# Two-layer memory attention with SwiGLU: attention matmuls issued in pairs on the two 64-row halves of the tensor array

## The chip, the cores and the metric

The kernel runs on one core of one Trainium2 chip. The metric is the device time of one execution in microseconds; the table below gives the runs of the kernel before. TensorE (PE) does the matmuls and writes into PSUM, which has eight banks of 128 partitions by 512 float32 columns. VectorE (DVE) and ScalarE (ACT) read PSUM, GpSimd (POOL) works on SBUF only, and SyncE (SP) issues nearly all DMAs. Every engine runs its own instructions in the order in which they were written; semaphores tie the engines together.

## The reference, cut to what matters

Two layers, each an attention block with a compressive memory and then a SwiGLU block, both with a layer norm before and the residual added after. S = 2048 rows, D = 512, H = 32 heads of 16, N = 4 segments of L = 512 rows, F = 1792.

```python
for s in range(N):
    qs, ks, vs = q[:, :, s], k[:, :, s], v[:, :, s]
    logits = jnp.einsum("bhqd,bhkd->bhqk", qs, ks) * scale + mask
    p = _softmax(logits, axis=-1)
    a_dot = jnp.einsum("bhqk,bhkd->bhqd", p, vs)
    pq = phi(qs)
    num = jnp.einsum("bhld,bhde->bhle", pq, M)
    den = jnp.einsum("bhld,bhd->bhl", pq, z)[..., None] + 1e-6
    o = g * (num / den) + (1.0 - g) * a_dot
    pk = phi(ks)
    M = M + jnp.einsum("bhld,bhle->bhde", pk, vs)
    z = z + jnp.einsum("bhld->bhd", pk)
```

## The kernel before, in words

**Precision.** Each float32 operand is split into a high part and a remainder, both held as fp32r. A product is the sum of three: high by high, high by remainder, remainder by high.

**Units.** An attention layer has 32 units: 4 segments, 4 groups of 8 heads, and the even or the odd four heads of the group. A unit does the following.

- `load3` (L513) brings q and k of the unit from DRAM scratch. Four heads lie as two pairs: index `j` picks partitions 0 to 47 or 64 to 111, index `p` a slot in the free dimension. The 48 partitions are the three terms of the split, 16 dimensions each. `cq` has four slots `2*j+p` in which the other half's partitions stay zero; `ck` has two.
- `mx_units` (L545) computes logits with queries on the partitions, to get the row maxima. Per head it fills three banks: 256+256 columns for query tiles 0 and 1, 384 for tile 2, 512 for tile 3. All 127 partitions take part, and since `cq` is zero in the other half, one matmul gives one head. DVE reduces each block with the causal mask (L564) into `mx`. `fin` transposes `mx` on PE (L573), ACT negates it into `nm` (L575), and a DMA on ACT's queue writes it to partition 127 of `cq`, against a partition of ones in `ck`.
- `at_units` (L585): `lt` computes the transposed logits (keys on the partitions) for 10 blocks of key tile by query tile, two matmuls of 256 columns each (L609). ACT takes the exponential (L615), POOL masks the four diagonal blocks (L619). `pv` multiplies by v on four 32-column quarters of the array, one per head (L636). `post` transposes and normalises on DVE.

**The other attention work on PE.** `mm3` (L298) issues the 12 matmuls of 128x512 of one tile (L295); it serves `qk_proj` (L481), `v_proj` (L465) and `wo_proj` (L732). `ln_transpose` (L384) transposes a normalised row tile in four matmuls (L387). `mem_read` (L682), `mem_update` (L702) and the end of `post` have memory products and transposes of their own (L690, L706, L667).

**SwiGLU.** `ffn` (L847) does the first block of weight columns directly (`up`, L1007; for row blocks 0 and 1 already during the attention), and the others by a Strassen scheme: `strassen` (L1029, matmuls at L1047) and `down` (L1084, matmuls at L1091).

**What sets the order.** Nothing is issued when it is described. Each call records an operation with its engine, a cost, what it reads and writes, and a priority. `issue` (L151) then replays them: the engine that can start earliest by the recorded costs takes its ready operation with the lowest priority number. Priorities come from tables of offsets (`OFF`, `PRE`, `EP`) and step constants. `bank` takes one of the eight PSUM banks when an operation first needs it; `CAP` limits how many banks each class of user may hold. `DRAIN` is what the replay adds where PE changes between full-array and quarter operations.

## Time and profile before

| | us |
|---|---|
| median of 3 runs | 1878.33 |
| lowest and highest run | 1873.25, 1881.59 |
| the profiled execution, its own time | 1878.99 |
| span of the profiled execution (first to last instruction) | 1877.2 |
| PE busy in the span | 1825.3 |
| DVE busy | 1407.5 |
| ACT busy | 873.1 |
| POOL busy | 918.9 |

Busy time is the time in which at least one instruction of the engine was under way. Matmuls overlap in the pipeline, so the length of one matmul (some 400 ns for 512 columns) is not its cost; the distance from one start to the next is. In the profile's views PE is the matmul, PEld the weight load, x is a count, and an arrow names what ended an idle time.

### The profile page before, as it was taken

The numbers are of one execution on the slowest core, as the hardware profiler recorded it, in microseconds if no ns is written. First come the engines' busy times: TensorE is split into PE (matmuls) and PEld (weight loads), VectorE is DVE, ScalarE is ACT, GpSimd is POOL, SyncE is SP. The second block draws the span as 40 slices with busy tenths as digits, with TensorE's granted clock in tenths as the row PEclk, the third lists the DMA queues.
The fourth block names the chain that finished last, engine by engine and source line by source line (L and its number), as shares of the span: only waits on it lengthen the run. The fifth ranks groups of instructions, "written<-read, shape, count | busy, mean of one in ns | idle before, by whom it ended". The sixth has DMA issues, their size and how long they took to land.

```text
span 1877.2 us, 33021 instructions
## 1 busy us (share of the span) xinstructions
PE 1825.3 (97%) x11360; PEld 1450.6 (77%) x11360; DVE 1407.5 (75%) x3834; ACT 873.1 (47%) x1629; POOL 918.9 (49%) x1186
## 2 busy tenths in 40 slices
PE   7999999999999999999989999999999999999999
PEld 5787787877778887788867877778777788878887
DVE  6878788778876678766776777787898766796656
ACT  4565564555533432433345655556454433333432
POOL 6344444444655654647533444444446647445551
PEclk9999999999999999999999999999999999999999
DMA  7535444464232132111373353455642311312121
GB/s 236 148 102 147 135 133 144 144 214 119 74 119 61 46 91 89 52 50 57 114 217 101 106 163 115 130 167 140 188 124 74 123 51 56 94 64 57 44 58 45
DMA packets 126967, 206.14 MB, mean 110 GB/s; under 512 B 14160, under 2 KB 52048, under 8 KB 126800
## 3 DMA queue, kind: packets, MB, share of 16 engines
q1 hardware_dynamic: 124752, 203.49, 36.7%
q8 instruction: 91, 1.49, 0.3%
q10 hardware_dynamic: 2048, 0.53, 0.1%
q14 instruction: 76, 0.62, 0.1%
HBM read 136.34 MB, written 67.11 MB: 108 GB/s over the span
## 4 chain that ended last, share of the span: by engine, by line
PE 48%; DVE 7%; issue 2%; DMA 2%; POOL 1%; ACT 1%; SPq 0%; DVEq 0%; POOLq 0%; ACTq 0%
PE ps L1047 18%; PE ps L1091 10%; PE ps L295 7%; PE ps L636 3%; PE ps L558 3%; PE ps L609 3%; DVE junk L564 2%; DMA s<-nm 1%; PE ps L1017 1%; DVE tt L961 1%; DVE s L983 1%; DVE s L1096 1%; PE ps L387 1%; DVE mx L564 0%; DVE of L961 0%
## 5 line engine op out<-in xcount | busy, mean ns | idle before, releaser
L1047 PE MATMUL ps<-s,s 128*128 128x512 f32 x2016 | 547.3, 396 | 9.5 <-ACT s L982 4.6
L295 PE MATMUL ps<-s,s 128*128 128x512 f32 x1536 | 526.2, 407 | 2.7 <-ACT s L451 1.2
L564 DVE CUSTOM_DVE_ANT_0 junk<-ps,amask 128x128 bf16<-128x128 f32 (+3 forms) x1024 | 433.5, 484 | 46.5 <-PE ps L558 45.1
L1047 PEld LDWEIGHTS ps<-s,s 128*128 128x128 f32 x2016 | 376.7, 188 | 106.0 <-ACT s L982 6.7
L1091 PE MATMUL ps<-s,vt 128*128 128x512 f32 x1296 | 378.0, 397 | 2.2 <-ACT vt L1003 2.2
L295 PEld LDWEIGHTS ps<-s,s 128*128 128x128 f32 x1536 | 287.2, 191 | 51.6 <-issue 6.1
L615 ACT ACTIVATE s<-ps 128x512 f32<-128x512 f32 x448 | 253.9, 609 | 108.5 <-PE ps L609 97.2
L1091 PEld LDWEIGHTS ps<-s,vt 128*128 128x128 f32 x1296 | 245.2, 189 | 58.6 <-ACT vt L1003 2.6
L558 PE MATMUL ps<-ck,s 127*128 127x256 f32 (+2 forms) x1024 | 276.6, 334 | 5.7 <-DMA ck<-scrk 4.9
L609 PE MATMUL ps<-s,ck 128*128 128x256 f32 x1280 | 250.6, 287 | 6.4 <-DMA s<-nm 4.5
L609 PEld LDWEIGHTS ps<-s,ck 128*128 128x128 f32 x1280 | 221.3, 189 | 38.3 <-issue 4.9
L1096 DVE TENSOR_TENSOR s<-s,ps 128x512 f32<-128x512 f32 x224 | 150.1, 683 | 92.0 <-PE ps L1091 91.7
L619 POOL TENSOR_SCALAR_AFFINE_SELECT s<-s 128x512 f32<-128x512 f32 x192 | 126.8, 663 | 171.9 <-ACT s L615 166.6
L558 PEld LDWEIGHTS ps<-ck,s 127*128 127x128 f32 x1024 | 177.6, 189 | 28.8 <-issue 6.4
L914 POOL TENSOR_TENSOR s<-mem,s 128x512 fp32r<-128x512 f32 x96 | 130.7, 1362 | 0.0
L492 POOL TENSOR_SCALAR s<-raw 128x512 fp32r<-128x512 f32 x64 | 45.4, 709 | 173.9 <-ACT raw L491 163.6
L1017 PE MATMUL ps<-s,s 128*128 128x512 f32 x384 | 123.9, 400 | 0.9 <-ACT s L391 0.9
L921 POOL COPY turn<-vt 128x1 f32<-128x1 f32 x20 | 3.7, 186 | 235.6 <-DVE vt L1004 235.6
L636 PE MATMUL ps<-s,vt 128*32 128x384 f32 (+3 forms) x1536 | 115.7, 419 | 0.1
L636 PEld LDWEIGHTS ps<-s,vt 128*32 128x32 f32 x1536 | 43.3, 109 | 64.1 <-issue 46.2
L615 ACT ACTIVATE pc<-ps 128x512 f32<-128x512 f32 x128 | 78.7, 615 | 19.9 <-PE ps L609 19.3
L494 POOL TENSOR_TENSOR s<-raw,s 128x512 fp32r<-128x512 f32 x64 | 84.3, 1317 | 4.3
(172 smaller groups left out, 2585.3 us busy)
## 6 DMA issues: line engine op xcount, KB each, us to landing
s<-scrq SPq DMA_DIRECT2D x128, 192.0 KB, 3.5
ck<-scrk SPq DMA_DIRECT2D x128, 192.0 KB, 4.5
scrq<-s SPq DMA_DIRECT2D x32, 512.0 KB, 3.6
scrk<-s SPq DMA_DIRECT2D x32, 512.0 KB, 3.3
scrq<-s SPq DMA_DIRECT2D x32, 256.0 KB, 3.2
scrk<-s SPq DMA_DIRECT2D x32, 256.0 KB, 2.5
s<-xmid SPq DMA_DIRECT2D x32, 256.0 KB, 5.2
xin<-xmid SPq DMA_DIRECT2D x32, 256.0 KB, 2.7
```

What stands on the lines that cost most here:

```text
L295: pe(n, passes, lambda: nc.tensor.matmul(view(ps.ap), lhsT=av(a.ap), rhs=bv(b.ap), start=start, stop=stop), [(a, rk[0]), (b, rk[1])], [ps])
L558: nc.tensor.matmul(ps.ap[:, a * 256:a * 256 + nk], lhsT=cq.ap[0:127, 2 * j + p, qt * 128:(qt + 1) * 128], rhs=ck.ap[0:127, p, 0:nk], start ...
L564: dve(w, lambda a=a, qt=qt, w=w, ps=ps, junk=junks[qt % 2]: nc.vector.tensor_tensor_reduce(out=junk.ap[:, :w], in0=ps.ap[:, a * 256:a * 25 ...
L609: nc.tensor.matmul(ps.ap[:, 256 * p:256 * p + 256], lhsT=ck.ap[:, p, kt * 128:kt * 128 + 128], rhs=cq.ap.rearrange("r (j p) c -> r p j c", ...
L615: act(512, lambda: nc.scalar.activation(view().rearrange("p x i c -> p (x i c)"), ps.ap, AF.Exp, scale=SCALE), [ps], [(Pb, key)], table="exp")
L619: gp(0.593, lambda: nc.gpsimd.affine_select(out=view()[:, 0], in_=view()[:, 0], pattern=[[0, 4], [1, 128]], compare_op=OP.is_ge, fill=0.0, ...
L636: nc.tensor.matmul(ps.ap[32 * i:32 * i + 32, qt * 128:(qt + k) * 128], lhsT=vt.ap[:, kt, VW * hd:VW * hd + 32], rhs=view(k=k)[:, :, idx], ...
L914: gp(n / 400, lambda hi=hi, lo=lo, src=src: nc.gpsimd.tensor_sub(lo(), src(), hi().bitcast(F32)), [read, (wt, (o0, 0))], [(wt, (o0, 1))])
L1017: pe(512, 1, lambda i=i, j=j, kc=kc, x=x, ps=ps, wt=wt: nc.tensor.matmul(ps.ap, lhsT=wt.ap[:, i, kc, cs], rhs=XT[b][j].ap[:, :, kc], start ...
L1047: pe(512, 1, lambda i=i, kc=kc, x=x, buf=buf, view=view: nc.tensor.matmul(ps.ap, lhsT=w.ap[:, o, i, kc], rhs=view(buf.ap, kc), start=(x == 0),
L1091: pe(512, 1, lambda i=i, j=j, fi=fi, x=x, ps=ps, wt=wt, cs=cs: nc.tensor.matmul(ps.ap, lhsT=ht.ap[:, 0:2048].rearrange("p (f a c) -> p f a ...
L1096: dve(512, lambda ps=ps, t=t: nc.vector.tensor_add(xb.ap[:, t, :], xb.ap[:, t, :], ps.ap), [ps, (xb, t)], [(xb, t)])
```

## The change

**Logits.** One tile per unit (`cqk`, `[128, 2, 2, 512]`) now holds q and k; the partitions 0 to 47 hold one head and 64 to 111 another, and nothing is zero-padded. Each matmul uses only 48 or 49 partitions of one half, and the matmuls come in pairs, the lower half for head `j=0` into one bank and the upper half for `j=1` into another. The rows of maxima go to partitions 48 and 112 of q, against -1 in k, so ACT copies `mx` without a sign. Transposed logits are cut by key tile, from the diagonal to column 512.

**Projections.** `mm_pair` takes two tiles at once (q and k of a group, or two row tiles of v or of the output). Twelve pair-steps use rows 0 to 63 for the first tile and 64 to 127 for the second; then the halves change places for twelve more. Between the two passes stands a hand-off: an ACT instruction that does nothing waits for the last matmul of the first pass, and the first matmul of the second pass waits for it. The same hand-off stands between the two transposes of `fin`. The first direct block of SwiGLU columns for row blocks 0 and 1 goes through `mm_pair` too.

**Transposes and the memory product** work on 64-row halves, two banks at once. `CAP`, the offsets, and the step constants are new, and `DRAIN` has entries for the halves ("lanes"); the replay's rule for banks counts several of one class in one operation.

```diff
-CAP = {'pj': 3, 'plt': 3, 'pmx': 3, 'ppv': 3, 'ff': 6, 'st': 6}
+CAP = {'pj': 4, 'plt': 4, 'pmx': 4, 'ppv': 2, 'ff': 6, 'st': 6}
...
-DRAIN = {("full", "cols"): 0.097, ("cols", "full"): 0.147}
+DRAIN = {("full", "cols"): 0.097, ("cols", "full"): 0.147, ("full", "lanes"): 0.2, ("lanes", "full"): 0.2,
+         ("lanes", "cols"): 0.096, ("cols", "lanes"): 0.22}
...
+    HALF = ((0, 64), (64, 128))
...
+    def mm_pair(ps, seqs):
+        got = {}
+        for ph in range(2):
+            n = len(seqs[0])
+            for x in range(n):
...
+                def go(x=x, ph=ph):
+                    for lane in range(2):
+                        q = lane ^ ph
+                        a, _, av, b, _, bv = seqs[q][x]
+                        r0, r1 = HALF[lane]
+                        o = nc.tensor.matmul(ps[q].ap, lhsT=av(a.ap)[r0:r1], rhs=bv(b.ap)[r0:r1],
+                                             start=(ph == 0 and x == 0), stop=(ph == 1 and x == n - 1))
+                        if ph == 1 and x == 0 and lane == 0:
+                            fence(o, got["turn"], "halves")
+                    got["last"] = o
+                pe(512, 1, go, rd, list(ps), mode="lanes", cost=0.229)
...
+                def bounce():
+                    got["turn"] = nc.scalar.nop()
+                    fence(got["turn"], got["last"], "halves")
+                turn = op("act", 0.06, bounce)
...
         def mx_units(u):
...
+            def part(cost, blocks):
+                ps = [bank("pmx"), bank("pmx")]
+                def fill():
+                    for p, qt, c0 in blocks:
+                        nk = 128 * (qt + 1)
+                        for j in range(2):
+                            nc.tensor.matmul(ps[j].ap[:, c0:c0 + nk],
+                                             lhsT=cqk.ap[64 * j:64 * j + 48, 0, p, qt * 128:(qt + 1) * 128],
+                                             rhs=cqk.ap[64 * j:64 * j + 48, 1, p, 0:nk], start=True, stop=True)
...
+            return [lambda p=p: part(0.232, ((p, 3, 0),)) for p in range(2)] + \
+                [lambda p=p: part(0.235, ((p, 2, 0), (p, 0, 384))) for p in range(2)] + \
+                [lambda: part(0.29, ((0, 1, 0), (1, 1, 256))), fin]
...
+            def part(b, cost, blocks, outs):
+                ps, Pb = [bank("plt"), bank("plt")], p_of(b)
+                def fill():
+                    for p, kt, c0 in blocks:
+                        nq = 512 - 128 * kt
+                        for j in range(2):
+                            nc.tensor.matmul(ps[j].ap[:, c0:c0 + nq],
+                                             lhsT=cqk.ap[64 * j:64 * j + 49, 1, p, kt * 128:(kt + 1) * 128],
+                                             rhs=cqk.ap[64 * j:64 * j + 49, 0, p, 128 * kt:512], start=True, stop=True)
```

**How the order moves.** The first place is PE in the middle of layer 0, where a unit's logits stand among projections. Before (L609 transposed logits, L558 logits for the maxima, L295 a projection; ps is a PSUM bank, s a large SBUF tile, ck the k tile):

```order
L609 MATMUL ps_4305<-s_211,ck_222 128x256 x2
L295 MATMUL ps_4266<-s_2665,s_120 128x512
L558 MATMUL ps_4312<-ck_90,s_67 128x256 x2
L558 MATMUL ps_4316<-ck_90,s_67 128x384
L558 MATMUL ps_4318<-ck_90,s_67 128x512
```

After (L615 logits for the maxima, L308 a projection, L632 the two transposes of `fin`):

```order
L308 MATMUL ps_4014<-s_230,s_3053 128x512
L615 MATMUL ps_4130<-s_238 128x384
L615 MATMUL ps_4131<-s_238 128x384
L615 MATMUL ps_4130<-s_238 128x128
L615 MATMUL ps_4131<-s_238 128x128
L632 MATMUL ps_4139<-ident,mx_578 16x64 x2
L308 MATMUL ps_4151<-s_3346,s_106 128x512
L308 MATMUL ps_4152<-s_3346,s_113 128x512
```

Five matmuls for one head's maxima and one block of another product have become pairs on two banks each; every projection step is two matmuls.

The second place is PE at a hand-off between the two passes of a projection (L308); the wait on ACT's sequencer is the hand-off, and L774 is the memory product:

```order
L308 MATMUL ps_2673<-s_1113,s_106 128x512
L308 MATMUL ps_2674<-s_1113,s_113 128x512
L615 MATMUL ps_2751<-s_67 128x256 [waits DMAHW7_49,DMAHW5_49,DVE_49]
L615 MATMUL ps_2752<-s_67 128x256 [waits DMAHW6_49,DMAHW1_49,DVE_49]
L308 MATMUL ps_2674<-s_1102,s_113 128x512 [waits Activation_sequencer_49]
L308 MATMUL ps_2673<-s_1102,s_106 128x512
L774 MATMUL ps_2763<-mb_265,phiq_2435 128x68 [waits Activation_49]
```

Four matmuls, two pair-steps, stand between the end of the first pass and the wait. Of the 72 paired projections 15 have nothing between, 8 up to one step, 25 about two steps, and the others three or more. Of the 64 in `fin`, 4 have nothing between, 4 one step, 13 two, the others more.

The third place is PE where layer 0's attention gives way to SwiGLU. Before (L295 the output projection, L1017 and L1047 SwiGLU):

```order
L295 MATMUL ps_6889<-s_238,s_5838 128x512
L1017 MATMUL ps_6896<-s_6483,s_4848 128x512
L295 MATMUL ps_6889<-s_224,s_5860 128x512
L1017 MATMUL ps_6929<-s_6480,s_5000 128x512
L1047 MATMUL ps_6886<-s_6766,s_6251 128x512
```

After (L308 pairs on halves, L1157 the Strassen products on the full array):

```order
L308 MATMUL ps_7703<-s_240,s_6664 128x512
L1157 MATMUL ps_7790<-s_7650,s_7027 128x512
L308 MATMUL ps_7702<-s_240,s_6664 128x512
L308 MATMUL ps_7703<-s_240,s_6664 128x512
L1157 MATMUL ps_7790<-s_7650,s_7027 128x512
L308 MATMUL ps_7702<-s_230,s_6679 128x512
```

The two kinds still alternate, but each alternation is now a change between halves and the full array. In the whole order PE changes from halves to the full array 55 times and back 55 times, and between halves and quarters 64 times each way; before, it changed between the full array and quarters 64 times each way. Inside SwiGLU the sequence of products is nearly the one before.

More of the change, by code (lines that the diff above doesn't have):

```diff
@@ L187, in issue @@
                             fr = sorted(free[tag])[:len(new)]
-                            if len(fr) < len(new) or not all(turn[b.cls] for b in new):
+                            many = [(c, [b.cls for b in new].count(c)) for c in {b.cls for b in new}]
+                            if len(fr) < len(new) or any(len(turn[c]) < k for c, k in many):
                                 heapq.heappop(n)
@@ L191, in issue @@
                                 continue
-                            when = max([fr[-1][0]] + [min(turn[b.cls]) for b in new])
+                            when = max([fr[-1][0]] + [sorted(turn[c])[k - 1] for c, k in many])
                             if when > t[e] + 1e-9:
@@ L316, in infini_swiglu @@
     bet = sb("bet", [128, NG, 2])
+    mxs = [sb(f"mx_{i}", [128, 16]) for i in range(2)]
     Mb = [sb(f"mb{n}", [128, 8, VW]) for n in range(NG)]
@@ L642, in pv @@
                 del MU[:]
-                pe(1280 + 100 * len(MU_), 4, go, [(vt, c) for c in range(8)] + reads + [e[1] for e in MU_],
-                   [ps] + [e[2] for e in MU_], mode="cols")
+                pe(1280 + 100 * len(MU_), 4, go, [(vt, c) for c in range(8)] + [f_[b] for b in range(3)] +
+                   [e[1] for e in MU_], [ps] + [e[2] for e in MU_], mode="cols")
                 for _, _, pm in MU_:
@@ L675, in post, with second, first, third @@
                        [of, (th, n)], [(tl, n)])
-            units = [lt(0, q) for q in range(4)] + [lt(1, q) for q in (1, 2, 3)]
-            units += [lt(2, 2), lt(3, 3), lt(2, 3), pv]
-            units.append(post)
-            return units
+            def second(p):
+                part(1, 0.235, ((p, 1, 0), (p, 3, 384)), (p,))
+                if p:
+                    tri(1, 0)
+                    tri(1, 384)
+            def first(p):
+                part(0, 0.232, ((p, 0, 0),), (p,))
+                if p:
+                    tri(0, 0)
+            def third():
+                part(2, 0.29, ((0, 2, 0), (1, 2, 256)), (0, 1))
+                tri(2, 0)
+            return [lambda p=p: first(p) for p in range(2)] + [lambda p=p: second(p) for p in range(2)] + \
+                [third, pv, post]
         def mem_read(s, n):
@@ L765, in attention @@
             at(-2.05)
-            for t in range(4):
-                ln_fin(0, t, "st")
+            for p in range(2):
+                ln_fin(0, p, "st")
         else:
```

463 lines of the change are left out of this document (251 added, 212 removed).

## The prediction

> **What bounds the kernel now.** I read the stretches of the span first, then the groups by line, then the timeline of one unit. The windows below are start, attention of layer 0, SwiGLU, attention of layer 1, SwiGLU; the columns are length, then busy time of PE, PEld, DVE, ACT and POOL.
>
> ```profile
> 0.00:52.00 52.00, 37.10 (x155) 29.12 (x155) 35.61 (x109) 22.68 (x39) 28.36 (x50) 0.97 0.78 232
> 52.00:456.00 404.00, 398.67 (x3344) 316.84 (x3345) 317.87 (x1231) 225.92 (x446) 173.32 (x262) 1.00 0.49 144
> 456.00:985.00 529.00, 513.19 (x2366) 409.22 (x2365) 390.96 (x717) 213.74 (x378) 295.59 (x335) 0.99 0.29 88
> 985.00:1425.00 440.00, 432.15 (x3586) 340.21 (x3584) 341.62 (x1295) 249.35 (x484) 192.73 (x297) 1.00 0.47 134
> 1425.00:1877.20 452.20, 444.15 (x1918) 355.24 (x1916) 321.45 (x488) 161.37 (x283) 228.86 (x245) 1.00 0.22 67
> 430.00:450.00 20.00, 19.10 (x143) 15.11 (x139) 18.79 (x85) 7.76 (x17) 4.37 (x6) 1.00 0.41 106
> ```
>
> In the two attention windows, 844 us together, PE is busy for 830.8 (98.4%) and DVE for 659.5 (78%). PE bounds them, and DVE is the next engine, with a fifth of slack. The last row is the one stretch I found where both are loaded: DVE 94%, PE 95.5%.
>
> ```profile
> L564 DVE CUSTOM_DVE_ANT_0 junk<-ps,amask 128x128 bf16<-128x128 f32 (+3 forms) x1024 | 433.5, 484 | 46.5 <-PE ps L558 45.1 <-issue 0.2
> L558 PE MATMUL ps<-ck,s 127*128 127x256 f32 (+2 forms) x1024 | 276.6, 334 | 5.7 <-DMA ck<-scrk 4.9 <-issue 0.2 <-ACT s L391 0.2
> L609 PE MATMUL ps<-s,ck 128*128 128x256 f32 x1280 | 250.6, 287 | 6.4 <-DMA s<-nm 4.5 <-DVE mx L564 0.6 <-ACT s L615 0.6
> ```
>
> The logits (L558, L609) are the work on PE that the change shrinks, and the idle time before them is 12 us in all: PE is not waiting for inputs there, it is computing. The maxima on DVE (L564), 433.5 us in the whole span, stay as they are.
>
> **Logits.** PE in the middle of a unit, start and length:
>
> ```profile
> 435.94 0.40 PE L558 MATMUL ps<-ck,s 127*128 127x256 f32 x2
> 436.18 0.40 PE L295 MATMUL ps<-s,s 128*128 128x512 f32 x1
> 436.41 0.34 PE L558 MATMUL ps<-ck,s 127*128 127x384 f32 x1
> 436.59 0.65 PE L609 MATMUL ps<-s,ck 128*128 128x256 f32 x4
> 437.07 0.40 PE L558 MATMUL ps<-ck,s 127*128 127x512 f32 x1
> 437.30 0.40 PE L609 MATMUL ps<-s,ck 128*128 128x256 f32 x2
> ```
>
> From start to start, two matmuls of 256 columns cost 0.24 us, 384 columns 0.18, 512 columns 0.23. The maxima of a head cost 0.24 + 0.18 + 0.23 = 0.65, of four heads 2.6; the ten transposed blocks cost 0.24 each, 2.4. That is 5.0 us for each of 64 units, 320 in all. After the change either product of a unit is five pair-fills per two banks: two of 512 columns, two of 384+128, one of 256+256. If the two halves run side by side, a pair costs what one matmul of its columns costs here: 2 x 0.23, 2 x (0.18 + 0.06, the 128 columns as a third of 384), and 0.24, so 1.18 per product, 2.36 per unit, 151 in all. The saving is 169 us.
>
> No row of before shows two row halves. The nearest are the column quarters of p times v:
>
> ```profile
> 198.22 0.39 PE L295 MATMUL ps<-s,s 128*128 128x512 f32 x1
> 198.54 1.93 PE L636 MATMUL ps<-s,vt 128*32 128x512 f32 x24
> 199.00 0.13 PEld L636 LDWEIGHTS ps<-s,vt 128*32 128x32 f32 x4 [0.30 <-issue]
> 200.29 0.61 PE L636 MATMUL ps<-pc,vt 128*32 128x256 f32 x8
> 200.83 0.50 PE L295 MATMUL ps<-s,s 128*128 128x512 f32 x1
> 201.17 0.40 PE L609 MATMUL ps<-s,ck 128*128 128x256 f32 x2
> L636 PEld LDWEIGHTS ps<-pc,vt x512: 110/110/110, 64.9 to 1424.0; 128*32 128x32 f32 x171
> ```
>
> Four heads of 512+384+128+256 = 1280 float32 columns each are done in 2.29 us (198.54 to 200.83). A float32 product on the whole array costs 0.23 for 136 columns (L690, below), so one head alone would need 2.2 and four in turn 8.7. And four weight loads of 0.11 us each lie within 0.13. So quarters run side by side, their loads too, and I take the same for halves. Bounds: side by side saves 169; wholly in turn, the logits cost 4.72 per unit (a saving of 18), and the projections, whose 72 x 24 = 1728 matmuls become as many pair-steps, cost 1728 x 0.23 = 397 more. Between them: if only the two halves' weight loads went in turn, at the 0.11 that a transposing matmul with its own load costs here (0.44 for four, below), a pair of 512 would still fit into 0.23, but the six two-block fills of a unit would take 0.44 instead of 0.24, 6 x 0.20 x 64 = 77 us.
>
> [...]
>
> **Projections, transposes.** A pair-step of 512 columns replaces a matmul of 512: nothing gained or lost. The transposes of 48 row tiles and 48 memory tiles, and 24 memory reads, are narrower:
>
> ```profile
> 202.57 0.39 PE L690 MATMUL ps<-mb,phiq 128*128 128x136 f32 x2
> 202.80 0.60 PE L387 MATMUL ps<-ident,xn 128*128 128x128 f32 x4
> 203.13 0.27 PE L387 MATMUL ps<-ident,xn 128*128 128x128 f32 x1
> 203.24 0.40 PE L690 MATMUL ps<-mb,phiq 128*128 128x136 f32 x2
> 203.57 0.60 ACT L391 CAST s<-ps 128x512 fp32r<-128x512 f32 x1
> 204.34 0.36 PE L558 MATMUL ps<-ck,s 127*128 127x256 f32 x1 [0.23 <-ACT s L391]
> ```
>
> A tile costs 0.44; on halves between 0.22 and 0.44, and I take the middle: 96 x 0.11 = 11 saved. A memory read has four products of 0.23 = 0.92; between 0.46 and 0.92, I take 0.6, 24 x 0.3 = 7. The second transpose of `fin` adds 0.05 x 64 = 3. Net saving 15.
>
> **Mode changes.** Going into quarters costs 198.22 to 198.54, 0.09 over the usual 0.23; coming out, 200.83 to 201.17, 0.11 over. There are as many after as before: nothing. The 110 changes between halves and the full array, where the layers join, are new. At most each shows the whole of a matmul and a load (0.40 + 0.19 - 0.23 = 0.36), at least 0.1 as for quarters; I take 0.15, near the row: 16 us (11 to 40).
>
> **Hand-offs.** In the rows above PE ends a transpose at 203.40, ACT starts at 203.57 and ends at 204.17, PE starts at 204.34: 0.17 each way. A hand-off shows a matmul's tail (0.40 - 0.23 = 0.17), 0.17, the empty instruction (0.05, an estimate) and 0.17: 0.56 us. What covers it is the pair-steps between, at 0.23. With the counts of the order (19 with none at 0.56, 12 with one at 0.33, 38 with two at 0.1) that is 10.6 + 4.0 + 3.8 = 18 us; uncovered, all 136 (72 + 64) would cost 76. Queued behind the empty instruction are ACT's exponentials; ACT is busy for 56% of these windows, so that alone costs nothing.
>
> **Sum.** PE loses 169 + 15 - 16 - 18 = 150 us of work. Of the 1024 matmuls of L558, 939 lie in the two attention windows:
>
> ```profile
> 52.00:456.00 404.00, 125.64 (x469) 80.88 (x469) 1.00 0.49 144
> 985.00:1425.00 440.00, 127.54 (x470) 81.30 (x469) 1.00 0.47 134
> ```
>
> That is 92%, so about 138 of the 150 fall there: PE needs 830.8 - 138 = 693 us. DVE needs its 659.5 and some 4 for adds cut in two: 664, or 96% of PE. The slack is gone, and DVE is late next. PE will not stay at 98.4%. With the row 430 to 450 as a guide I take 94.5%: 693 / 0.945 = 733, a saving of 111. Of the 12 us outside the windows I take 5. SwiGLU is bound by PE on products whose order hardly changes: nothing. The span becomes 1877.2 - 116 = 1761; the execution takes 1.8 us more than its span, as in the profiled execution (1878.99), which stands within 1 us of the median of the runs. Forecast: **1763 us**. With PE at 98% the windows take 707, at 90% 770: its own range is 1735 to 1800.
>
> **Rivals.**
>
> 1. *Banks and DVE hold the stage.* Every pair takes two banks at once, a maxima pair keeps them while DVE works off both, and a projection holds two for its whole length, 24 steps, where one tile held one for 12. If PE fills only 87%, the windows take 797, the span 1830 less 5: 1827. For it: DVE at 96% of PE leaves no room to catch up. Against it: the maxima's waits for PE are 45 us in total now, so DVE is mostly fed early, and eight banks remain. 14%.
> 2. *The halves' weight loads go in turn:* 77 us more on PE, 770 at 96% is 802: 1832. Against it: the loads of the quarters. 9%.
> 3. *The other side: a pair costs clearly more than one matmul,* because the halves do not stream side by side or because the next load of a half waits for it. The change has 1728 + 1024 = 2752 pairs, so it loses from 150 / 2752 = 0.055 us per pair on, that is, when a pair of 512 takes 0.285 instead of 0.23. Wholly in turn: 1877 + 397 - 18 - 15 + 34 = 2275; a load of 0.19 exposed on each pair: 1877 + 2752 x 0.19 - 150 = 2250; a pair at 0.30: 1877 + 2752 x 0.07 - 150, about 1920. For it: nothing in the trace shows rows of the array divided. Against it: the quarters. 10%. [...]
> 4. *DVE gets denser than its busy time says,* since back-to-back instructions overlap, and PE stays at 98%: 707, and all 12 outside: 1728. 5%.
>
> **Chances.** Forecast 62%, the rivals 14, 9, 10, 5. What a measurement of this kernel can tell from no change is about 0.5%, 9 us. Faster by more than that: all but rival 3 and a few hundredths of the hand-offs piling up, 0.88; within, 0.02; slower, 0.10. The range 1722 to 1832 holds the forecast and rivals 1, 2 and 4, and leaves out rival 3 and the ends; its lower end is rival 4 less the difference between 0.15 and 0.1 per mode change.
>
> **What would show it.** Pairs of 512 on halves starting every 0.23 us, four matmuls of 256+256 in 0.24; PE's total busy near 1675; the attention windows 365 us each, with DVE above 88% in them; gaps on PE before the first matmul of a second pass of at most 0.6 us and 20 us in all; SwiGLU's products on PE as close together as before. Wrong would be: pair starts above 0.28, PE waiting for DVE or ACT for over 100 us, or hand-offs of over a microsecond because ACT is behind.

## The result and the profile after

The change made the kernel slower. The median of 4 runs is 1990.08 us (1988.01 to 1996.67), against 1879.26 us (1873.25 to 1881.59, 4 runs) before on the same chip: a ratio of 1.060 with a 95% interval of 1.0565 to 1.0636. The profiled execution took 1988.01 us, with a span of 1986.0 us.

First the stretches of the changed kernel: attention of layer 0, SwiGLU, attention of layer 1, SwiGLU (length, busy time of PE, PEld, DVE, ACT and POOL with counts, then the granted clock, the DMA share and GB/s).

```profile
52.00:512.00 460.00, 418.47 (x4135) 291.70 (x4133) 365.43 (x1332) 236.78 (x481) 187.10 (x290) 0.91 0.45 132
512.00:1030.00 518.00, 505.96 (x2386) 386.13 (x2383) 351.14 (x615) 193.63 (x341) 255.50 (x300) 0.97 0.26 80
1030.00:1530.00 500.00, 454.29 (x4444) 325.67 (x4442) 388.47 (x1354) 257.54 (x511) 199.24 (x306) 0.89 0.44 126
1530.00:1986.00 456.00, 438.80 (x1975) 351.22 (x1973) 307.04 (x471) 159.63 (x281) 221.03 (x244) 0.99 0.21 65
```

The two attention windows have grown from 844 to 960 us. Three things in these rows are new. PE is idle for 87 us in them (460.00 - 418.47 and 500.00 - 454.29), where it was idle for 13. The granted clock (the share of TensorE's full clock that it was given) is 0.91 and 0.89, where it was 1.00: some 95 us of the two windows are lost to that. And DVE is busy for 754 us, not 660.

The groups of the page (busy, mean ns, idle before and who ended it) name the engine that is late:

```profile
L622 DVE CUSTOM_DVE_ANT_0 junk<-ps,amask 128x256 bf16<-128x256 f32 (+3 forms) x1024 | 492.4, 487 | 115.3 <-PE ps L615 50.0
L308 PE MATMUL ps<-s,s 64*128 64x512 f32 x3456 | 602.7, 430 | 12.5 <-DVE mx L622 4.2
L615 PE MATMUL ps<-s 48*128 48x384 f32 (+3 forms) x1024 | 206.5, 369 | 26.4 <-DVE mx L622 18.3
L615 PEld LDWEIGHTS ps<-s 48*128 48x128 f32 x1024 | 133.8, 207 | 75.5 <-DVE mx L622 50.1
```

The 1024 reductions of the maxima (L622, formerly L564) have the same mean length as before, 487 ns against 484, but keep DVE busy for 492.4 us instead of 433.5. DVE also stands idle before them for 115.3 us instead of 46.5, and PE names only 50.0 of that. The timeline of DVE shows why (start, length). Before, at 311.37 us, and then after, at 300.29 us; the short instruction behind each reduction (0.08 us) is by its name the read-out of its accumulator:

```profile
311.37 0.69 DVE L564 CUSTOM_DVE_ANT_0 junk<-ps,amask 128x512 bf16<-128x512 f32 x1
311.98 0.08 DVE L564 DVE_READ_ACCUMULATOR2_ANT mx<- 128x1 f32 x1
311.98 0.28 DVE L564 CUSTOM_DVE_ANT_0 junk<-ps,amask 128x128 bf16<-128x128 f32 x1
312.19 0.08 DVE L564 DVE_READ_ACCUMULATOR2_ANT mx<- 128x1 f32 x1
312.19 0.42 DVE L564 CUSTOM_DVE_ANT_0 junk<-ps,amask 128x256 bf16<-128x256 f32 x1
```

```profile
300.29 0.69 DVE L622 CUSTOM_DVE_ANT_0 junk<-ps,amask 128x512 bf16<-128x512 f32 x1
300.90 0.08 DVE L622 DVE_READ_ACCUMULATOR2_ANT mx<- 128x1 f32 x1
301.12 0.69 DVE L622 CUSTOM_DVE_ANT_0 junk<-ps,amask 128x512 bf16<-128x512 f32 x1
301.74 0.08 DVE L622 DVE_READ_ACCUMULATOR2_ANT mx<- 128x1 f32 x1
301.74 0.25 DVE L784 SCALAR_TENSOR_TENSOR rm<-ps,ginv 128x16 f32<-128x16 f32 x2
```

Before, a reduction of 512 columns is 0.69 us long and gives way to the next after 0.61 us, so the next one starts 0.08 us before its end. After, the next one starts 0.83 us later, 0.14 us after the end. These are no odd places: where one reduction directly follows another of 512 columns, the median distance of the starts is 0.61 us before and 0.84 after. The instructions say what it waits for. The reduction also writes its full result, which nobody reads, into one of two buffers, `junks[qt % 2]`. Before, neighbouring reductions were of query tiles 0, 1, 2, 3, so the buffers took turns; after, the neighbours are two heads with the same `qt`, or tiles 2 and 0. Two neighbours in the changed kernel's order, with their semaphores:

```
L622 ISA junk_577,mx_657<-ps_732,amask 128x512 [waits DVE_49,PE_49]
L622 ISA junk_577,mx_657<-ps_733,amask 128x512 [waits DVE_49,PE_49]
```

The second waits on DVE's own semaphore until the first has written `junk_577`. The replay that makes the order does not see this: the buffer is entered under a key that differs for every reduction.

The clock is the second thing. The stretch around one fall of the granted clock, in the same columns as above, and what PE was waiting for in it:

```profile
330.00:336.80 6.80, 6.75 (x80) 4.48 (x78) 6.33 (x25) 0.93 (x2) 4.77 (x9) 1.00 0.47 118
336.80:340.20 3.40, 2.45 (x14) 1.02 (x11) 3.15 (x15) 2.23 (x4) 2.60 (x4) 0.99 0.62 202
340.20:353.80 13.60, 11.84 (x71) 8.53 (x70) 12.21 (x45) 6.99 (x16) 2.31 (x3) 0.50 0.27 107
353.80:361.00 7.20, 6.75 (x95) 4.35 (x93) 4.12 (x15) 4.22 (x10) 5.41 (x10) 1.00 0.59 138
```

```profile
337.39 0.18 PEld L615 LDWEIGHTS ps<-s 48*128 48x128 f32 x1 [0.34 <-DVE mx L622]
338.81 0.22 PE L632 MATMUL ps<-ident,mx 64*16 64x64 f32 x1 [0.29 <-DVE mx L622]
339.85 0.56 PE L615 MATMUL ps<-s 48*128 48x512 f32 x1 [0.53 <-DVE mx L622]
```

Between 336.8 and 340.2 PE is busy for 2.45 us of 3.40, much of it with the ends of matmuls that stand alone (14, with 1.02 us of weight loads), because the maxima are late. Then the granted clock is 0.50 for 13.6 us, four times 3.41, and every fall that ends within these traces lasts a whole number of times 3.41 us. There are 32 such stretches in the changed kernel, 222 us together, and 4 before, 17 us together.

For all runs below the same account of the attention is used, from the first to the last p times v of each layer, both layers added. It comes from the stretches of the profile: the length, the time in which PE is idle, the length times (1 - granted clock), and what is left, taken as PE's work at full clock. "Outside" is the rest of the span. The account has two limits. Idle time inside a stretch at half clock is in part counted twice, 6 us in the changed kernel. And a matmul that stands alone is busy to its end, some 0.4 us where its pace is 0.23, so waits between matmuls appear in part as work. The change by itself:

| | length | PE idle | lost to the clock | PE work | outside |
|---|---|---|---|---|---|
| before | 850.8 | 12.6 | 1.7 | 836.5 | 1026.4 |
| after | 934.2 | 82.1 | 88.7 | 763.4 | 1051.8 |

So the work on PE did shrink, by 73 us in this account, and 69 us of idle time, 87 of clock and 25 outside took its place.

### The profile page after: what moved, and what is told of

Read it like the earlier page. It is cut to its first block, busy times and chain, and to the rows that moved or that the text cites. A ratio compares the mean times of both kernels' runs of the same rounds, so it can differ in the third digit from the quotient of the medians.

```text
span 1986.0 us, 36543 instructions
## 1 busy us (share of the span) xinstructions
PE 1852.5 (93%) x13216; PEld 1381.2 (70%) x13216; DVE 1443.2 (73%) x3858; ACT 869.3 (44%) x1653; POOL 883.4 (44%) x1177
## 4 chain that ended last, share of the span: by engine, by line
PE 45%; DVE 10%; issue 3%; ACT 1%; POOL 1%; DMA 1%; SPq 0%; DVEq 0%; ACTq 0%; POOLq 0%
PE ps L1157 17%; PE ps L1201 11%; PE ps L308 9%; DVE junk L622 5%; PE ps L699 3%; PE ps L615 2%; PE ps L672 2%; PE ps L1130 1%; PE ps L774 1%; DMA s<-nm 0%; ACT s L678 0%; DVE tt L716 0%; DMA xmid<-phiq 0%; DVE vt L1110 0%; DVE Y L720 0%
## 5 line engine op out<-in xcount | busy, mean ns | idle before, releaser
L308 PE MATMUL ps<-s,s 64*128 64x512 f32 x3456 | 602.7, 430 | 12.5 <-DVE mx L622 4.2
L622 DVE CUSTOM_DVE_ANT_0 junk<-ps,amask 128x256 bf16<-128x256 f32 (+3 forms) x1024 | 492.4, 487 | 115.3 <-PE ps L615 50.0
L1157 PE MATMUL ps<-s,s 128*128 128x512 f32 x2016 | 541.5, 400 | 13.2 <-ACT s L1088 3.5
L1157 PEld LDWEIGHTS ps<-s,s 128*128 128x128 f32 x2016 | 377.0, 189 | 121.3 <-issue 9.3
L308 PEld LDWEIGHTS ps<-s,s 64*128 64x128 f32 x3456 | 392.9, 197 | 79.4 <-issue 22.1
L615 PE MATMUL ps<-s 48*128 48x384 f32 (+3 forms) x1024 | 206.5, 369 | 26.4 <-DVE mx L622 18.3
L672 PE MATMUL ps<-s 49*128 49x128 f32 (+3 forms) x1024 | 183.6, 349 | 19.7 <-DVE mx L622 9.0
L615 PEld LDWEIGHTS ps<-s 48*128 48x128 f32 x1024 | 133.8, 207 | 75.5 <-DVE mx L622 50.1
L672 PEld LDWEIGHTS ps<-s 49*128 49x128 f32 x1024 | 125.6, 198 | 59.7 <-DVE mx L622 26.6
L699 PE MATMUL ps<-s,vt 128*32 128x128 f32 (+2 forms) x1280 | 110.3, 477 | 2.5 <-DVE mx L622 1.1
```

Source lines behind the costliest of these rows:

```text
L308: o = nc.tensor.matmul(ps[q].ap, lhsT=av(a.ap)[r0:r1], rhs=bv(b.ap)[r0:r1], start=(ph == 0 and x == 0), stop=(ph == 1 and x == n - 1))
L615: nc.tensor.matmul(ps[j].ap[:, c0:c0 + nk], lhsT=cqk.ap[64 * j:64 * j + 48, 0, p, qt * 128:(qt + 1) * 128], rhs=cqk.ap[64 * j:64 * j + 48, ...
L622: dve(w, lambda j=j, w=w, c0=c0, x=x, junk=junks[qt % 2]: nc.vector.tensor_tensor_reduce(out=junk.ap[:, :w], in0=ps[j].ap[:, c0:c0 + w], i ...
L672: nc.tensor.matmul(ps[j].ap[:, c0:c0 + nq], lhsT=cqk.ap[64 * j:64 * j + 49, 1, p, kt * 128:(kt + 1) * 128], rhs=cqk.ap[64 * j:64 * j + 49, ...
L699: nc.tensor.matmul(ps.ap[32 * i:32 * i + 32, 128 * kt:512], lhsT=vt.ap[:, kt, VW * hd:VW * hd + 32], rhs=f_[b].ap[:, i, c0:c1], start=(x = ...
L1157: pe(512, 1, lambda i=i, kc=kc, x=x, buf=buf, view=view: nc.tensor.matmul(ps.ap, lhsT=w.ap[:, o, i, kc], rhs=view(buf.ap, kc), start=(x == 0),
```

## The experiments

Where a run has an interval, it is the ratio to the kernel before, whose median over the runs beside these was 1878 to 1879 us.

**e1_junk: the unused buffers by turns.**

```diff
-    junks = [sb(f"junk_{i}", [128, 384 + 128 * i], BF16) for i in range(2)]
+    junks = [sb(f"junk_{i}", [128, 512], BF16) for i in range(2)]
+    turns = [0]
...
+                        def peak(j=j, w=w, c0=c0, x=x):
+                            junk = junks[turns[0] % 2]
+                            turns[0] += 1
```

> The changed kernel, with one edit: the unused full-size result of the row-maximum reduction on VectorE goes to two buffers in turn instead of to the buffer that the query tile's parity names. The order of all engines is the same. Theory A (VectorE): in the changed kernel neighbouring reductions have query tiles of the same parity, so each waits until the one before has finished writing the same unused buffer; starts of 512-column reductions are 0.83 us apart there, 0.61 before. If that is what starves TensorE, the starts fall back to about 0.62 us, the granted clock rises from 0.944 to above 0.985, and the time falls from 1990 to 1780 to 1840 us, below the 1879 of before. Rival B (the halves themselves): if TensorE's clock falls because half-array matmuls count as little work, or because hand-offs and mode changes stop it, the clock stays below 0.96 and the time above 1930. Rival C (PSUM banks): if pairs of banks are what is short, the time stays above 1930 with VectorE's starts at 0.62 and long waits of VectorE for TensorE.

Measured: 1918.87 us (1915.87 to 1922.09), ratio 1.021 (1.0186 to 1.0234). Nothing else differs from the changed kernel, so the buffer alone cost 71 of the 111 us. The group of the maxima is back at the time of before:

```profile
L626 DVE CUSTOM_DVE_ANT_0 junk<-ps,amask 128x256 bf16<-128x256 f32 (+3 forms) x1024 | 442.0, 484 | 64.3 <-PE ps L616 63.2 <-issue 0.3
```

Here PE names 63.2 of the 64.3 us of idle time; nothing unnamed is left. The starts of reductions of 512 columns are back at 0.61 us (median). But the kernel is still 40 us above before, so the buffer is not the whole cause, and no theory had the number: theory A had 1780 to 1840 us at a clock above 0.985, rivals B and C had above 1930. The clock is 0.954, which is rival B's sign (below 0.96).

**e2_before_onejunk: the same wait put into the kernel before.**

```diff
-                            dve(w, lambda a=a, qt=qt, w=w, ps=ps, junk=junks[qt % 2]: nc.vector.tensor_tensor_reduce(
+                            dve(w, lambda a=a, qt=qt, w=w, ps=ps, junk=junks[1]: nc.vector.tensor_tensor_reduce(
```

> The kernel before, with one edit: all row-maximum reductions write their unused result to one buffer instead of to two in turn. Theory A: each of the 1024 reductions then waits for its predecessor, 0.12 to 0.22 us, some 120 to 220 us more on VectorE, which was busy for 660 of the 844 us of the attention windows; VectorE becomes the bound and the time goes from 1879 to between 1900 and 1970 us. Rivals B and C: the reduction's buffer does not matter, 1879 within 10 us.

Measured: 2017.22 us (2014.24 to 2018.39), ratio 1.0729 (1.0702 to 1.0757). With one buffer for all, the kernel before loses 139 us, more than the 21 to 91 expected. Its group, and its two stretches from the first to the last p times v:

```profile
L564 DVE CUSTOM_DVE_ANT_0 junk<-ps,amask 128x128 bf16<-128x128 f32 (+3 forms) x1024 | 501.2, 489 | 137.1 <-PE ps L558 38.7 <-DVE mx L564 0.9 <-PE ps L609 0.5
```

```profile
71.00:565.30 494.30, 452.82 (x3548) 339.10 (x3550) 370.50 (x1291) 250.27 (x481) 190.48 (x294) 0.98 0.41 120
1085.10:1562.60 477.50, 438.98 (x3505) 329.04 (x3508) 358.17 (x1245) 248.49 (x475) 189.04 (x292) 0.99 0.42 122
```

The wait is shown from both sides. This run serves for the clock too: PE is idle for 80 us in its attention, as in the changed kernel (82), yet the clock costs it 12 us there, not 89.

**e3_short: e1_junk, with each reduction over the first 64 columns of its block.**

```diff
-    out=junk.ap[:, :w], in0=ps[j].ap[:, c0:c0 + w], in1=amask.ap[:, 512 - w:],
+    out=junk.ap[:, :64], in0=ps[j].ap[:, c0:c0 + 64], in1=amask.ap[:, 0:64],
```

> As the kernel with two buffers in turn, but each row-maximum reduction reads only the first 64 columns of its block, so the maximum left out of the softmax shift is that of the other columns; all instructions and their order stay. VectorE then does some 350 us less in the attention. Theory A with VectorE still the bound after the buffer edit: another 30 to 60 us below it. If after the buffer edit TensorE's own work (pairs, hand-offs, mode changes) is the bound: less than 15 us below it. The granted clock is above 0.985 in both.

Measured: 1895.34 us (1887.99 to 1898.59), ratio 1.0076 (1.005 to 1.0103). DVE's share of the attention falls from 79% to 55%, which gains 24 us: less than the 30 to 60 us expected if DVE is the bound, more than the 15 expected at most if PE's own work is. The clock is 0.955, where above 0.985 was expected. The kernel still does not reach the one before, so what remains is not DVE's load alone.

**e4_nohand: e1_junk without the hand-offs between the halves.**

```diff
-                        q = lane ^ ph
+                        q = lane
...
-                        if ph == 1 and x == 0 and lane == 0:
-                            fence(o, got["turn"], "halves")
...
-                    o = nc.tensor.transpose(ps.ap[0:16, r0:r1], mx.ap[r0:r1, :], ident.ap[r0:r1, r0:r1])
-                    if lane:
-                        fence(o, got[1], "halves")
+                    o = nc.tensor.transpose(ps.ap[0:16, r0:r1], mx.ap[0:64, :], ident.ap[0:64, 0:64])
```

> As the kernel with two buffers in turn, but without hand-offs: in the second pass of a pair each half of the array stays with its tile and multiplies the same 64 rows again, and both transposes of the row maxima read the first 64 queries; the empty ACT instructions stay and wait for nothing. The other half of the rows is left out of the projections. My prediction priced all hand-offs at 18 us: 10 to 25 us below the kernel with two buffers. If hand-offs are the main cost of the pairs (136 at 0.56 us or more): 60 us or more below it. If they are hidden: the same within 8 us.

Measured: 1914.56 us (1912.33 to 1916.79), ratio 1.0186 (1.0152 to 1.0221). By the medians all hand-offs together cost about 4 us; the two runs overlap those of e1_junk, so it is a few us at most, as expected if they are hidden. The trace of e1_junk agrees. Of its 72 hand-offs in projections 15 leave PE idle for 0.10 to 0.11 us before the second pass, two for 0.46 and 0.92, and the others not at all.

**e6_probe: the pace of pairs by itself.** One matmul or pair after the other, no input later than the first.

```python
def pair(widths=(512,), rhs=None, k=64):
    for w in widths:
        for lane in range(2):
            nc.tensor.matmul(ps[lane][:, at:at + w], lhsT=lhs(64 * lane, 64 * lane + k), rhs=b[64 * lane:64 * lane + k, 0:w], start=True, stop=True)
```

> A probe of TensorE alone: it computes nothing of the reference and copies rows of x to the output. Stretches of about 55 us: bursts of n matmuls of 512 columns on the whole array, n = 2, 3, 4, 6, each burst waiting for a copy on ScalarE of the last one's result (about 1.1 us of pause, so that the array streams some 31, 39, 46, 57% of the time); the same with bursts of n pairs on 64-row halves, n = 4, 6, 8, 12, 16 (46, 57, 63, 72, 78%); 220 pairs without a pause; then 30 steps each of one shape for their pace; then whole-array matmuls and pairs in turns of 1, 2 and 4. Before each stretch comes a stream of whole-array matmuls that gives the full clock back. Theory A (the clock counts the rows in use): with whole-array matmuls the clock falls for n = 2 and 3 only; with halves, at the same pause, it falls for n = 4, 6, 8 (23 to 32% by rows) and probably 12 (36%), is open for 16 (39%), and holds for pairs without a pause (50%). Theory B (only streaming time counts): halves with n = 4 and more hold the full clock as whole-array bursts of n = 4 do. Theory C (only the length of a pause counts): all stretches with pauses behave alike. Pace: a pair of 512 at 0.22 to 0.235 us, 384+128 and 256+256 at 0.24; if 256+256 is at 0.29 or more, the short blocks carry part of the lost 70 us within pairs. A change between halves and the whole array, 0.15 in the prediction: the stretch with turns of 1 then takes 24 x 2 x (0.23 + 0.15) = 18 us, turns of 4 12.8 us; at 0.3 a change 25 and 14.6.

The stretches with pauses told little of the edge, because the bursts overlapped the pauses. The clock fell in one of them only, whole-array bursts of 2; its mean over the run is 0.976. One thing they do show: theory A counted a pair as half the array and had pairs in bursts of 4, 6 and 8 lose the clock, and all of them held it (in bursts of 4 it had at most a third of a window by that count). The paces are clean. PE, start and length: the last whole-array matmuls before 220 pairs of 512, then these pairs; 30 times 384+128; 30 times 256+256; single steps by turns:

```profile
490.64 0.84 PE L44 MATMUL ps<-R 128*128 128x512 f32 x3
491.41 50.18 PE L55 MATMUL ps<-R 64*128 64x512 f32 x440
...
617.05 8.81 PE L55 MATMUL ps<-R 64*128 64x384 f32 x120
...
635.07 7.45 PE L55 MATMUL ps<-R 64*128 64x256 f32 x120
...
670.04 0.50 PE L55 MATMUL ps<-R 64*128 64x512 f32 x2
670.47 0.50 PE L44 MATMUL ps<-R 128*128 128x512 f32 x1
670.91 0.50 PE L55 MATMUL ps<-R 64*128 64x512 f32 x2
```

A pair of 512 takes 50.18 / 220 = 0.228 us, as much as one matmul on the whole array (0.225 from start to start in the first row): here the halves run side by side, and their weight loads, new ones for each matmul, add nothing that shows (from 495 to 535 us PE is busy for 40.00 us, and PEld for 33.08 with 354 loads). 256+256 takes 7.45 / 30 = 0.25. But 384+128 takes 8.81 / 30 = 0.29, not the 0.24 of the prediction. Two steps of different mode by turns start 0.43 apart, so a change costs 0.43 - 0.23 = 0.20 us. Out of a longer stream it is less: of the three matmuls from 490.64 the last starts at 491.09, and the first pair 0.32 later, 0.09 over the pace.

**e5_fullproj: e1_junk with the projections on the whole array.**

```diff
-                    for lane in range(2):
-                        q = lane ^ ph
-                        a, _, av, b, _, bv = seqs[q][x]
-                        r0, r1 = HALF[lane]
-                        o = nc.tensor.matmul(ps[q].ap, lhsT=av(a.ap)[r0:r1], rhs=bv(b.ap)[r0:r1], ...)
+                    a, _, av, b, _, bv = seqs[ph][x]
+                    o = nc.tensor.matmul(ps[ph].ap, lhsT=av(a.ap), rhs=bv(b.ap), start=(x == 0), stop=(x == n - 1))
```

> e1_junk with the projections on the whole array again: 24 matmuls of 128 rows in place of 24 pair-steps, no second pass on swapped halves and so no hand-off; logits, transposes and memory reads stay on halves, and the order of TensorE's work is the same. It has 1075 changes between halves and the whole array in place of 109. At the 0.20 us per change that the probe showed for a lone step, 966 x 0.20 = 193 us are added, less the hand-offs (4 us): 2070 to 2130. At the 0.15 of the prediction 145: 2060; if changes hide as in long streams (0.09) 87: 2000. With whole-array matmuls more rows stream, but the pauses of the changes take away as much of the time, so the clock is open; if it fell less, up to 76 us less.

Measured: 2058.08 us (2 runs), ratio 1.0954 (1.0917 to 1.0991). It is 139 us above e1_junk, 139 / 966 = 0.14 us for each added change. In the attention alone PE's work grew by 141 (table below), with 1011 changes in place of 8: 0.14 again, near the 0.15 of the prediction. It is why the projections are on halves at all: alone they gain nothing, but logits on halves between projections on the whole array would pay for two changes of 0.14 us each.

**e7_probe2: what the clock counts.** The probe again, computing nothing of the reference, with bursts and pauses kept apart.

```python
def duty(step, n, us=48.0):
    for _ in range(max(6, int(us / (0.23 * n + 1.2)))):
        for i in range(n):
            ps = step(rhs=True if i == 0 else None)
        nc.scalar.mul(G[:], ps[:], 0.5)
```

> The probe again, its instructions kept in the order written (in the first one the pauses were overlapped, so the array was in use for half the time or more in nearly every stretch). A burst of n steps of 0.23 us, then a pause of some 1.2 us for a copy on ScalarE: the array streams about 35, 41, 46, 50% of the time at n = 3, 4, 5, 6. Whole array at n = 3, 4, 5; pairs of halves at 3 to 6; pairs that use 48 of 64 rows at 5, 6; one half alone at 8 with pauses (60% of the time, 30% by rows) and without (94%, 47%); pairs with 16 of 64 rows without pauses (94%, 23%); four column quarters, and one quarter alone (94%, 23%). Theory A (the share of rows that stream counts): whole array falls at 3, holds at 5; pairs with both halves do the same; 48-row pairs fall at 5 and 6; one half falls with pauses; 16 rows and one quarter fall. Theory A2 (a half or quarter counts as in use whatever rows it has): 48-row pairs as 64-row pairs, 16 rows hold; one half falls with pauses. Theory B (only time in which anything streams counts): one half, 16 rows and one quarter hold, as whole-array bursts at the same share of time do. If the edge is at 0.40 +- 0.05 of the array for pairs as for the whole array, the halves have no fault of their own: the changed kernel's clock fell because the same time has less array work in it, and a pause takes it under the edge.

The stretches (length, PE, PEld, ACT, POOL, then the clock), in this order: whole array at n = 3 and 4; pairs at 3, 4 and 6; pairs of 48 rows at 6; one half with pauses, one half without; pairs of 16 rows without pauses; one column quarter without pauses. Each starts after the clock has fallen, where it fell.

```profile
27.00:61.00 34.00, 19.34 (x60) 9.70 (x60) 11.74 (x20) 0.00 (x0) 1.00 0.00 0
92.00:136.00 44.00, 32.43 (x64) 17.91 (x63) 9.22 (x16) 0.00 (x0) 0.50 0.00 0
232.00:269.00 37.00, 20.82 (x132) 10.69 (x132) 12.88 (x22) 0.00 (x0) 1.00 0.00 0
297.00:341.00 44.00, 32.42 (x128) 17.98 (x124) 9.16 (x16) 0.00 (x0) 0.50 0.00 0
444.00:481.00 37.00, 25.72 (x190) 16.21 (x186) 8.96 (x15) 0.00 (x0) 1.00 0.00 0
587.00:635.00 48.00, 38.07 (x158) 23.84 (x158) 7.87 (x14) 0.00 (x0) 0.50 0.00 0
659.00:716.00 57.00, 48.04 (x104) 31.56 (x102) 7.16 (x12) 0.00 (x0) 0.50 0.00 0
741.00:775.00 34.00, 34.00 (x151) 27.60 (x150) 0.00 (x0) 0.00 (x0) 1.00 0.00 0
799.00:867.00 68.00, 68.00 (x322) 52.74 (x320) 0.00 (x0) 0.00 (x0) 0.50 0.00 1
941.00:969.00 28.00, 28.00 (x67) 7.25 (x66) 0.00 (x0) 0.00 (x0) 1.00 0.00 1
```

Pairs with both halves running fare as the whole array here (at 3 the clock is 1.00, at 4 and 5 it is 0.50), so halves as such are no cause in these stretches. But rows count in them: the same bursts of 6 hold the clock with 64 rows per half (1.00) and lose it with 48 (0.50), and 16 rows lose it without any pause (0.50). So theories A2 and B are out. Columns did not count in the one stretch that asks: one quarter of them holds the clock (1.00 for 28 us; it ran on plain float32, the other stretches on fp32r). Theory A holds in the main point. It missed the bursts of 3, which hold the clock, those of 5, which lose it, and the quarter, which holds it.

So the average of a stretch does not decide here, since bursts of 3 have the lowest (PE is busy for 57 and 56% of them). All changes of the clock in a trace lie on one grid of 3.41 us, and I take each window of this grid as what counts. At n = 3 every window has two bursts, 6 x 0.228 = 1.37 us or 40% of it. At n = 4 and 5 windows differ, and those before the falls work out to 39 to 42%. The edge of these bursts lies there; this probe does not resolve why 40% held at n = 3.

With each matmul counted at that pace and by its share of the 128 rows, all falls in the traces of before (4), after (32), e1_junk (28) and e2_before_onejunk (11) follow a window at or below 41%; in each of the four traces at most 4 such windows, of some 480 to 560, did not lead to a fall. The rows matter to this. If each matmul on a half counts as the whole half, whatever rows it uses, 6 of the 28 windows before a fall in e1_junk and 8 of the 29 in e3_short come out above 41%, up to 48%; by rows none does.

**e8_rows64 and e9_short64: more rows in the logits.** Both products of the logits change in the same way; two fills of zeros on GpSimd per layer and buffer come with it.

```diff
-                                             lhsT=cqk.ap[64 * j:64 * j + 48, 0, p, qt * 128:(qt + 1) * 128],
-                                             rhs=cqk.ap[64 * j:64 * j + 48, 1, p, 0:nk], start=True, stop=True)
+                                             lhsT=cqk.ap[64 * j:64 * j + 64, 0, p, qt * 128:(qt + 1) * 128],
+                                             rhs=cqk.ap[64 * j:64 * j + 64, 1, p, 0:nk], start=True, stop=True)
...
```

> e1_junk with 64 instead of 48 or 49 rows in both products of the logits: the other rows of a query are zero, those of a key -1, and row 48 still holds the maxima of the buffer's last use, which shifts both products alike and leaves the softmax as it is. TensorE's order is that of e1_junk, and a matmul takes as long with 64 rows as with 48; two fills of zeros of 0.9 us per layer and buffer are added on GpSimd. Theory A (the clock follows the share of rows that stream): by e1_junk's trace 6 of its 28 falls of the clock had 64 rows lifted above 0.38, so 20 to 23 falls remain, the clock's loss in the attention windows goes from 76 to 50 to 70 us, and the time to 1895 to 1913. Theory B (only pauses count): 1916 to 1923, as e1_junk (1918.9), with 26 to 30 falls.

> e3_short (each maximum over the first 64 columns of its block alone) with the 64 rows of e8_rows64. Theory A: 7 of e3_short's 29 falls of the clock vanish, the loss goes from 65 to 40 to 58 us and the time from 1895.3 to 1873 to 1889. Theory B: 1891 to 1899, with 27 to 31 falls.

Measured: e8_rows64 1913.41 us (1912.5 to 1915.7), ratio 1.0188 (1.0162 to 1.0214); e9_short64 1885.05 us (1878.77 to 1890.3), ratio 1.0037 (1.0022 to 1.0052). Against e1_junk and e3_short they gain 5.5 and 10.3 us with the same products in the same order. The clock's loss in the attention falls from 75.9 to 61.4 and from 64.8 to 42.7 us. That is theory A's direction, and its loss in the attention. But the falls are 26 and 25 where it had 20 to 23 and 22; 26 is what theory B had for e8_rows64, and 1913.41 us is just above theory A's range. Over the whole span e8_rows64 hardly shows a gain in clock: the loss outside the attention rises from 13 to 25 us, and the sum goes from 89 to 87. In e9_short64 it goes from 86 to 66, in the attention alone, and its time is within theory A's range. So e9_short64 supports theory A, and e8_rows64 taken alone settles nothing. The stretches from first to last p times v of e1_junk, then of e8_rows64:

```profile
65.50:506.70 441.20, 410.84 (x4247) 296.47 (x4250) 342.55 (x1300) 241.09 (x490) 195.39 (x301) 0.92 0.46 134
1020.80:1456.30 435.50, 410.22 (x4248) 300.89 (x4252) 348.18 (x1318) 244.07 (x490) 191.67 (x295) 0.91 0.48 135
```

```profile
63.80:496.50 432.70, 406.46 (x4247) 293.32 (x4250) 342.36 (x1301) 241.39 (x491) 195.36 (x302) 0.93 0.46 137
1016.60:1446.10 429.50, 404.32 (x4251) 294.61 (x4252) 347.99 (x1317) 243.92 (x490) 191.64 (x295) 0.92 0.48 136
```

**The account of all.**

| | length | PE idle | lost to the clock | PE work | outside |
|---|---|---|---|---|---|
| e1_junk | 876.7 | 55.6 | 75.9 | 745.2 | 1043.6 |
| e2_before_onejunk | 971.8 | 80.0 | 11.9 | 879.9 | 1043.6 |
| e3_short | 850.1 | 48.0 | 64.8 | 737.3 | 1046.1 |
| e4_nohand | 868.8 | 52.9 | 73.8 | 742.1 | 1046.3 |
| e5_fullproj | 1023.0 | 39.3 | 97.5 | 886.2 | 1035.0 |
| e8_rows64 | 862.2 | 51.4 | 61.4 | 749.4 | 1048.6 |
| e9_short64 | 836.3 | 48.7 | 42.7 | 744.9 | 1044.7 |

These rows show the account's second limit: e2_before_onejunk has the matmuls of the kernel before, and its work comes out 43 us larger, because more of them stand alone. With the buffer mended, the change saves 91 us of PE's work and pays 43 in idle time, 74 in clock and 17 outside. No version that was run beats the kernel before.

## Why the prediction was wrong

The forecast was 1763 us in a range of 1722 to 1832; the time is 1990. The step that failed is the one on DVE.

- **"The maxima on DVE (L564), 433.5 us in the whole span, stay as they are"**, and the 664 us that follow from it. The instructions did stay; their spacing did not. 433.5 us for 1024 reductions of 484 ns, whose lengths add up to 496, says that neighbours overlap, and the change put an end to that by its order alone (at 512 columns and a length of 0.69 us, the starts went from 0.61 to 0.84 us apart). DVE needed 754 us in the windows, and nearly every reduction waited for the one before. This is 71 of the 111 us. The prediction had read in its rival 4 that back-to-back instructions overlap, and had not asked what lets them.
- **"PE will not stay at 98.4% ... I take 94.5%"** counted only idle time. In e1_junk PE is busy for 94% of the attention (821.1 of 876.7), near the forecast; the clock took 76 us more, which no term of the sum and no rival had. The changed kernel does the attention with less work on PE (763 us against 836 in the account), so it has less to stream in each 3.41 us, and the same pause weighs more: e2_before_onejunk has PE idle for 80 us and loses 12 to the clock, the changed kernel 82 and 89. That this is the reason is argued from these traces and the probe; no run held the clock up by itself. That rows count is shown in this case by the probe (bursts of 6 pairs at a clock of 1.00 with 64 rows, 0.50 with 48) and by the windows before the falls (8 of 29 in e3_short above 41% without the rows, none with them).
- **Logits, 169 us saved; net 138 in the attention.** The mechanism was right: halves run side by side, pairs of 512 start every 0.23 us, and rivals 2 and 3 (loads in turn, a pair above 0.285) are out. The size was off. PE's work fell by 73 us in the changed kernel and by 91 in e1_junk. Of the missing 47, the pairs of 384+128 are 4 x (0.29 - 0.24) x 64 = 13 us, since 128 columns were priced by their length alone. A part of the rest is matmuls that stand alone and count as work to their ends, as e2_before_onejunk shows; how much was not taken apart.
- **Mode changes at 0.15 us** were right: 0.14 in e5_fullproj, 0.20 for a lone step in the probe. That puts the 110 at 15 to 22 us. The 0.19 of a load, in the upper bound there and in rival 3, is the mean of L295's weight loads in the trace of before (191 ns).
- **Hand-offs, 18 us:** about 4. The counts were right, 15 projections with nothing between; the price was not. Such a hand-off takes mostly 0.49 to 0.56 us from one start to the next in e1_junk, where the pace is 0.23: some 0.3 and not 0.56. PE starts 0.05 us after the end of the empty instruction, where 0.17 was taken, and this instruction lasts 0.017, where 0.05 was taken without a row.
- **SwiGLU: nothing.** Outside the attention 25 us were lost (17 in e1_junk). The clock's loss there is 23 us after and 7 before, so most of the 25 is the same cause. In e1_junk it is 13, which explains 6 of the 17; the rest stays open.
- **Rival 1, banks and DVE hold the stage (1827 us),** came nearest in kind. It took DVE's time as fixed and had no price for the clock, so its number was far too low.

What the prediction named as signs: pair starts of 0.23 (seen), hand-offs below 0.6 (yes, but for one of 0.92), PE's total busy time near 1675 (1852.5), attention windows of 365 us with DVE above 88% in them (460 and 500, with 79 and 78%). DVE's busy share does not show that its instructions wait for each other: from the first to the last p times v it is 79% in the changed kernel and 79% in e1_junk.

## What to carry to other kernels

Before reordering, look at what neighbouring instructions share, unread outputs included; here DVE's 1024 reductions were busy for 433.5 us where their lengths add up to 496, and one shared scratch buffer ended that overlap (501.2 us in e2_before_onejunk). When matmuls are made cheaper while another engine keeps its pace, look at the granted clock in each window, not only at PE's busy share: here 80 us of idle time on PE cost 12 us of clock with the matmuls of before, and 82 us cost 89 with the cheaper ones. Price narrow blocks from a row of their own (a pair of 384+128 columns took 0.29 us, where its length alone gave 0.24).

## What the hardware showed that was not expected

- In the probe and in four traces the clock went by the rows that stream in a window of 3.41 us. Bursts of six pairs held it (1.00) at 64 rows per half and lost it (0.50) at 48; pairs of 16 rows lost it (0.50) without any pause; one half alone without pauses held it (1.00). The falls followed windows at or below 41%, counted by the share of the 128 rows in use.
- Short pauses were enough in windows that were thin otherwise: the largest pause of PE in e1_junk's attention was 2.3 us, and the clock fell 22 times there. The falls last 3.41 us and multiples of it, at a clock of 0.50.
- One column quarter with 128 rows, on plain float32, held the full clock (1.00) for 28 us, though it uses a quarter of the array as the pairs of 16 rows do, which lost it (0.50). It is one stretch of one run.
